# Attention and FFN on one core: scores in one tensor per head, products with v in a slot's fourth quarter, q turned while exp runs, VectorE's FFN work by quarters, the last exp behind the relus

## The chip, the cores and the metric

The kernel runs on 1 core of one Trainium2 chip. The metric is device microseconds of the whole program; three runs of the kernel before are shown.

## The reference

```python
scores = matmul(q, k.T) / 8                       # 8 batches x 8 heads, 576 x 576, head_dim 64
thresh = max(scores, -1) - tau
scores = where(scores >= thresh, scores, -1e9)
attn = exp(scores - max); attn /= sum(attn) + 1e-9
x = matmul(attn, v)                               # heads side by side: (8, 576, 512)
xn = (x - mean(x)) / sqrt(var(x) + 1e-6) * g_ln
out = x + relu(xn @ w_ch1) @ w_ch2                # 512 -> 2048 -> 512, all float32
```

## The kernel before, in words

The attention is cut into **slots**, 9 to a batch (`SLOTS`), 72 in all; `n` counts them, `s` is the slot's place in its batch. A slot holds two heads by 256 rows of q, that is four blocks of 128 x 576 scores. Slots `s` = 0 to 3 take the first 256 rows of the four pairs of heads, `s` = 4 (`HP`) the last 64 rows of all of them, `s` = 5 to 8 the second 256 rows. The **FFN** has 16 groups of 288 tokens, two to a batch. A group has 129 steps: 64 of the first product (16 tiles `p1`, 4 steps each, a relu on ScalarE behind every tile), one for the variance, 64 of the second (4 tiles `p2`, 16 steps each). A step is two matmuls in the program, four in the trace.

The order is written by hand (`manual_schedule`): each engine runs its instructions as the loop over `n` issues them. TensorE gets the slot's products with v (of slot n-2, `values_of`), its scores, and then FFN steps in four **quarters**; `second_part` deals steps to a quarter so that a group ends when the next is `ready`. `at_quarter` puts a call into a later quarter, and `run` makes the calls. `aside` holds VectorE's FFN work (the product of `p2` with `rb`, which frees the tile `p2`; the turning of the finished tile and its store), made by `run_aside`.

In a slot: VectorE takes the maxima (L339, two reduces of two blocks each), ScalarE four exps (L347), VectorE masks and sums (L354, four), GpSimd divides (L360, four). From the second batch on VectorE then turns 32 x 32 blocks (L430) into `et`, SyncE's queue writes `et` to DRAM (`scr`, L436) and `fetch` reads it back as `em` and `er` (L450, L453), the turned weights for the product with v. In the first batch TensorE turns the weights instead (`turn_weights`, L380). At the end of a slot `turn` prepares q and k of the next pair of heads (GpSimd L266, VectorE L269 to L281) and `load_qk` loads the pair after it into the one pair of input tiles. In slots up to the ninth `tick` also converts the FFN's weights, five pieces of work a slot.

PSUM has one tile `sc` of six banks, with the product with v in a corner of the third (`pv`), and two banks that `p1`, `p2`, `mean`, `var` and the turned weights share by turns (`ps_ff`). `product` (L99) issues most matmuls of the FFN.

Of the kernel before, what the change touches and what calls it, by code (L numbers as in the profile page):

```python
# [18 lines left out]
def kernel(  # L19
# [42 lines left out]
    QH = 256  # L62
# [226 lines left out]
    sc = ps_sc.tile([128, 6 * 512], F32, name="sc")  # L289
    pv = sc[:, 1024 + 128 : 1024 + 128 + QH]  # L290

    def block(i):
        return i // 2 * 3 * 512 + i % 2 * S
# [8 lines left out]
    def scores(b, s):  # L302


        if s == HP:
            for hp in range(HP):
                _, kT, qd = turned[b * HP + hp]
                first = block(hp)
                for at, n in span(first, S):
                    o = at - first  # L310
                    product(sc[:, at : at + n], lhsT=qd, rhs=kT[:, o : o + n], start=True, stop=True)
        else:
# [4 lines left out]
            for h in range(2):  # L317
                t = 0
                for j in range(2):
                    first = block(2 * h + j)  # L320
# [3 lines left out]
            for t, h, j, at, n, o in sorted(pieces):  # L324
                r = slice(64 * h, 64 * h + 64)
                nc.tensor.matmul(  # L326
                    sc[:, at : at + n], lhsT=qT[r, half, j * 128 : (j + 1) * 128],
# [3 lines left out]
    blocks = [sc[:, block(i) : block(i) + S] for i in range(4)]  # L331

    def exponentials():
# [40 lines left out]
    def turn_weights(s, es):  # L374

        em, er = turned_tiles()
        for i in range(4):
            tp = ps_ff.tile([128, J, 128], F32, tag="ff", name="tp")
# [32 lines left out]
        return em, er  # L411
# [185 lines left out]
    QUARTERS = 4  # L597
    STEPS = 1 + NK * ND * 2
# [58 lines left out]
    for n in range(NS):  # L657
# [83 lines left out]
```

## Time and profile before

| | |
|---|---|
| median of 3 runs (lowest to highest) | 1831.15 us (1830.4 to 1831.39) |
| the profiled execution: time, span | 1831.4 us, 1829.6 us |
| TensorE busy, mean granted clock | 81%, 0.92 |
| VectorE, ScalarE, GpSimd busy | 45%, 24%, 26% |
| DMA engines, share of the span in SyncE's and ScalarE's hardware queue (q1) | 46.0% |
| the scores of slots n = 0, 9, 16, 70, 71 begin at | 9.6, 243.6, 416.5, 1676.6, 1703.5 us |

The span is from the first to the last instruction; the profiled execution's time is 1.8 us longer. A batch of nine slots takes 209 to 211 us from the second batch on. In the timeline a number in brackets is the time that the engine stood idle before the row, with what ended it.

### The profile page before, as it was taken

Reading aid. Unit: us, or ns where it says so; the run is one execution under the profiler, and the core shown is the slowest. Engines: PE = TensorE matmul, PEld = TensorE weight load, DVE = VectorE, ACT = ScalarE, POOL = GpSimd, SP = SyncE. Lnnn points to the kernel's source line nnn. Section 1 sums busy time; section 2 is a strip of 40 time slices with the busy share of each in tenths; the row PEclk is TensorE's granted clock in tenths of the full one; section 3 lists DMA queues with packets and bytes.
Section 4 is the critical chain, followed back from the end, with each engine's and each line's share of the span. In section 5 each row is a group of like instructions: output and inputs, shape, how many; then the busy total and the mean of one; then the engine's idle time right before and its main releaser. Section 6 shows DMA issues by size and latency. Waiting matters only on the chain.

```text
span 1829.6 us, 29170 instructions
## 1 busy us (share of the span) xinstructions
PE 1489.3 (81%) x11704; PEld 862.9 (47%) x11704; DVE 818.2 (45%) x1380; ACT 444.7 (24%) x810; POOL 476.7 (26%) x735
## 2 busy tenths in 40 slices
PE   3635788888888788888888888888888888887898
PEld 2323444454544444445544544454544545454555
DVE  5557435353543535444454445444454534445210
ACT  3344422213122121322222131312212131221210
POOL 3565322121221212222221222222231222223110
PEclk7777789899999999999999999999999999999999
DMA  6322226444573446545464436645464445634400
GB/s 139 87 73 92 76 44 134 115 115 113 122 171 104 114 107 142 134 116 135 96 154 115 122 104 142 139 112 127 108 156 117 118 109 119 161 104 117 106 12 14
DMA packets 628023, 205.10 MB, mean 112 GB/s; under 512 B 535088, under 2 KB 623792, under 8 KB 627888
## 3 DMA queue, kind: packets, MB, share of 16 engines
q1 hardware_dynamic: 625488, 202.94, 46.0%
q8 instruction: 92, 1.51, 0.3%
q10 hardware_dynamic: 2368, 0.30, 0.1%
q14 instruction: 43, 0.35, 0.1%
q0 software_dynamic: 32, 0.00, 0.0%
HBM read 119.41 MB, written 83.76 MB: 111 GB/s over the span
## 4 chain that ended last, share of the span: by engine, by line
PE 69%; DVE 11%; ACT 10%; issue 4%; POOL 2%; DMA 2%; SPq 2%; ACTq 0%; DVEq 0%; POOLq 0%
PE p L99 49%; PE sc L326 8%; PE sc L478 8%; DVE neg L339 8%; ACT e L347 6%; DVE e L354 2%; PE sc L99 2%; ACT x L494 1%; ACT L347 1%; POOL e L360 1%; ACT hidden L567 1%; DMA er<-scr 1%; SPq L111 1%; DMA stage<-in_moe_w_ch_dram 1%; PE tp L380 1%
## 5 line engine op out<-in xcount | busy, mean ns | idle before, releaser
L99 PE MATMUL p<-xc,w 128*64 128x288 f32 x4096 | 533.4, 419 | 80.4 <-ACT hidden L567 79.0
L99 PE MATMUL p<-hidden,w 128*64 128x288 f32 x4096 | 547.7, 429 | 56.7 <-DVE o L534 30.5
L99 PEld LDWEIGHTS p<-hidden,w 128*64 128x64 f32 x4096 | 309.5, 145 | 283.7 <-issue 40.2
L99 PEld LDWEIGHTS p<-xc,w 128*64 128x64 f32 x4096 | 296.4, 141 | 303.2 <-ACT hidden L567 98.5
L339 DVE TENSOR_REDUCE neg<-sc 128x2 f32<-128x1152 f32 x144 | 188.8, 1353 | 411.5 <-PE sc L326 339.1
L354 DVE SCALAR_TENSOR_TENSOR e<-sc,thr,e 128x576 f32<-128x576 f32 x288 | 218.3, 815 | 212.8 <-ACT e L347 212.7
L360 POOL TENSOR_SCALAR e<-e,den 128x576 f32<-128x576 f32 x288 | 217.2, 770 | 346.7 <-DVE den L358 299.8
L347 ACT ACTIVATE e<-sc,neg 128x576 f32<-128x576 f32 x288 | 189.6, 741 | 324.0 <-DVE neg L339 323.8
L326 PE MATMUL sc<-kT,qT 64*128 64x512 f32 (+3 forms) x1024 | 161.2, 457 | 83.0 <-ACT x L494 37.4
L430 DVE STREAM_TRANSPOSE et<-e 128x1152 f32<-128x1152 f32 x112 | 151.8, 1368 | 56.0 <-POOL e L360 53.9
L567 ACT ACTIVATE hidden<-p 128x288 f32<-128x288 f32 x256 | 102.6, 416 | 305.0 <-PE p L99 305.0
L326 PEld LDWEIGHTS sc<-kT,qT 64*128 64x128 f32 x1024 | 89.3, 200 | 168.0 <-issue 67.6
L494 ACT COPY x<-sc 128x256 f32<-128x256 f32 x64 | 23.8, 372 | 510.7 <-PE sc L478 510.7
L478 PE MATMUL sc<-em,v_in 128*64 128x256 f32 (+1 forms) x1536 | 144.9, 333 | 0.0
L342 POOL TENSOR_SCALAR thr<-neg,low_sb 128x2 f32<-128x2 f32 x144 | 40.8, 283 | 328.8 <-DVE neg L339 328.8
L478 PEld LDWEIGHTS sc<-em,v_in 128*64 128x64 f32 x1536 | 94.0, 140 | 44.0 <-issue 3.6
L535 POOL TENSOR_TENSOR o<-o,x 128x288 f32<-128x288 f32 x64 | 51.0, 796 | 226.1 <-DVE o L534 226.1
L534 DVE TENSOR_TENSOR o<-p,rb 128x288 f32<-128x288 f32 x64 | 28.2, 441 | 139.0 <-PE p L99 138.8
L503 POOL TENSOR_TENSOR sum<-sum,x 128x256 f32<-128x256 f32 (+1 forms) x64 | 31.6, 494 | 182.5 <-ACT x L494 180.0
L380 PE MATMUL tp<-ident,e 128*128 128x128 f32 x144 | 31.4, 379 | 57.8 <-ACT em L389 51.7
L579 DVE RECIPROCAL rb<-rb 128x288 f32<-128x288 f32 x16 | 31.0, 1939 | 73.3 <-ACT rb L578 73.3
L503 POOL TENSOR_TENSOR sum<-x 128x256 f32<-128x256 f32 (+1 forms) x32 | 15.7, 491 | 156.1 <-ACT x L494 135.5
(71 smaller groups left out, 704.1 us busy)
## 6 DMA issues: line engine op xcount, KB each, us to landing
scr<-et SPq DMA_DIRECT2D x224, 288.0 KB, 5.1
em<-scr SPq DMA_DIRECT2D x112, 512.0 KB, 5.0
stage<-in_moe_w_ch_dram SPq DMA_DIRECT2D x22, 512.0 KB, 3.8
q_in<-in_q_dram SPq DMA_DIRECT2D x128, 72.0 KB, 3.3
out_dram<-ot SPq DMA_DIRECT2D x256, 36.0 KB, 1.7
k_in<-in_k_dram SPq DMA_DIRECT2D x124, 72.0 KB, 2.5
v_in<-in_v_dram SPq DMA_DIRECT2D x64, 128.0 KB, 2.6
scr_rest<-et SPq DMA_DIRECT2D x28, 288.0 KB, 4.9
```

Of the source, the lines that this page charges most:

```text
L99: nc.tensor.matmul(out[r], lhsT=lhsT[:, r], rhs=rhs, **flags)
L326: nc.tensor.matmul(sc[:, at : at + n], lhsT=qT[r, half, j * 128 : (j + 1) * 128], rhs=kT[r, o : o + n], start=True, stop=True,)
L339: nc.vector.tensor_reduce(out=neg[:, i : i + 2], in_=sc[:, block(i) : block(i) + 2 * S].rearrange("p (j n) -> p j n", j=2), axis=AXL.X, op ...
L347: nc.scalar.activation(es[:, i], blocks[i], func=AF.Exp, bias=neg[:, i : i + 1])
L354: nc.vector.scalar_tensor_tensor(out=es[:, i], in0=blocks[i], scalar=thr[:, i : i + 1], in1=es[:, i], op0=ALU.is_ge, op1=ALU.mult, accum_o ...
L360: nc.gpsimd.tensor_scalar(out=es[:, i], in0=es[:, i], scalar1=den[:, i : i + 1], scalar2=1.0, op0=ALU.mult, op1=ALU.mult,)
L380: nc.tensor.transpose(tp[:, c], es[:, i, c * 128 : (c + 1) * 128], ident)
L430: nc.vector.transpose(et[:, h].rearrange("p n j c -> p j n c"), es[:, 2 * h : 2 * h + 2].rearrange("p j (n c) -> p j n c", c=32),)
L478: nc.tensor.matmul(dst[64 * h : 64 * h + 64], lhsT=vt[:, c, h, :] if c < J else vr[:, h, :], rhs=rhs, start=(c == 0), stop=(c == J),)
L503: nc.gpsimd.tensor_tensor(out=sums[g][:, cols], in0=x[:, 0, cols] if c == 1 else sums[g][:, cols], in1=x[:, c, cols], op=ALU.add,)
L535: nc.gpsimd.tensor_tensor(out=o, in0=o, in1=groups[g][:, m], op=ALU.add)
L567: nc.scalar.activation(hidden[:, d], p1, func=AF.Relu)
```

## The change

Nothing is added to the arithmetic, and no instruction is taken away. Four things move:

1. The scores lie in two PSUM tiles of three banks, one per head of the slot, so that waits are per head.
2. `exponentials` stops ahead of the fourth exp. The FFN steps of the first quarter, with their relus, are issued ahead of that exp, and `turn` of the next pair and a `run_aside` follow it.
3. `values_of` of slot n-1 is issued at the start of the fourth quarter of slot n (before: of slot n-2 ahead of slot n's scores), and `fetch` moves from the second quarter to the first. `turn_weights` is cut in two.
4. The quarters get shares of 0.6, 1, 1 and 0.6 (`ROOM`); `centre` moves to quarter 1, and `ready` is one quarter earlier.

In SyncE's queue `load_qk` follows the slot's `scr` writes, as before; `fetch` follows these loads, and one store of a finished FFN tile that stood ahead of it in some slots now stands behind it.

```diff
-    sc = ps_sc.tile([128, 6 * 512], F32, name="sc")
-    pv = sc[:, 1024 + 128 : 1024 + 128 + QH]
+    sc = [ps_sc.tile([128, 3 * 512], F32, name=f"sc{i}") for i in range(2)]
+    pv = sc[0][:, 2 * S : 2 * S + QH]
+    blocks = [sc[i // 2][:, i % 2 * S : i % 2 * S + S] for i in range(4)]
...
         for i in range(4):
+            if i == 3:
+                yield es, thr
             nc.scalar.activation(es[:, i], blocks[i], func=AF.Exp, bias=neg[:, i : i + 1])
...
         for i in range(4):
+            if i == 2:
+                yield
             tp = ps_ff.tile([128, J, 128], F32, tag="ff", name="tp")
...
+    ROOM = (0.6, 1.0, 1.0, 0.6)
...
-        return QUARTERS * (b * SLOTS + (HP, 2 * HP)[t] + 2) + 3
+        return QUARTERS * (b * SLOTS + (HP, 2 * HP)[t] + 2) + 2
...
-        owed += ((g + 1) * STEPS - issued) / left if left > 0 else 8
+        owed += ((g + 1) * STEPS - issued) * ROOM[i] / left if left > 0 else 8
...
-        at_quarter(n, 2, centre, g)
+        at_quarter(n, 1, centre, g)
...
         tick(0)
+        scores(b, s)
         run(n, -1)
-        scores(b, s)
-        es, thr = exponentials()
-        tick(1)
+        rest = exponentials()
+        es, thr = next(rest)
         run(n, 0)
         second_part(n, 0)
+        next(rest, None)
+        u = (n + 1) // SLOTS * HP + (n + 1) % SLOTS
+        if (n + 1) % SLOTS < HP and u < len(units):
+            turn(u)
+        run_aside()
+        tick(1)
         run(n, 1)
         second_part(n, 1)
         weights(es, thr)
...
-            at_quarter(n + 1, 1, lambda s=s, scr=scr, box=box: box.append(fetch(s, scr)))
+            at_quarter(n + 1, 0, lambda s=s, scr=scr, box=box: box.append(fetch(s, scr)))
         else:
-            at_quarter(n + 1, 0, lambda s=s, es=es, box=box: box.append(turn_weights(s, es)))
+            made = turn_weights(s, es)
+            at_quarter(n + 1, -1, next, made)
+            at_quarter(n + 1, 0, lambda made=made, box=box: box.append(next(made)))
-        at_quarter(n + 2, -1, lambda b=b, s=s, box=box: values_of(b, s, box[0]))
+        at_quarter(n + 1, 3, lambda b=b, s=s, box=box: values_of(b, s, box[0]))
...
-        u = (n + 1) // SLOTS * HP + (n + 1) % SLOTS
-        if (n + 1) % SLOTS < HP and u < len(units):
-            turn(u)
-            if u + 1 < len(units):
-                load_qk(u + 1)
+        if (n + 1) % SLOTS < HP and u + 1 < len(units):
+            load_qk(u + 1)
+        run(n, 3)
```

The first place is ScalarE's order in slot `s` = 2 of a batch. `x` is the copy of the product with v, `e` the exps, `hidden` the relus, `p_` a tile `p1`. Before:

```order
L494 COPY x<-sc 128x256
L347 ACTIVATE e<-sc,neg 128x576 x4
L567 ACTIVATE hidden<-p_5878 128x288
L578 ACT_TABLE_LOAD
L578 ACTIVATE rb<-var,eps_sb 128x288
```

and now (`sc_150` and `sc_151` are the two heads' tiles):

```order
L348 ACTIVATE e<-sc_150,neg 128x576 x2
L348 ACTIVATE e<-sc_151,neg 128x576
L569 ACTIVATE hidden<-p_5730 128x288
L348 ACTIVATE e<-sc_151,neg 128x576
L569 ACTIVATE hidden<-p_5770 128x288
```

One relu now stands ahead of the fourth exp, and the copy of x no longer stands ahead of the exps.

The second place is VectorE's order in slot `s` = 1, from the maxima to the turned weights (`kT`, `qT`, `q_diag` are `turn`, `xc` is `centre`). Before:

```order
L339 TENSOR_REDUCE neg<-sc 128x2 x2
L354 SCALAR_TENSOR_TENSOR e,den<-sc,thr,e 128x576 x4
L358 RECIPROCAL den<-den 128x4
L540 STREAM_TRANSPOSE ot<-o 128x288
L534 TENSOR_TENSOR o<-p_5503,rb 128x288
L518 TENSOR_TENSOR xc<-x,mean 128x288 x4
L430 STREAM_TRANSPOSE et<-e 128x2x18x32 x2
L269 STREAM_TRANSPOSE kT<-k_in 128x576
L273 STREAM_TRANSPOSE qT<-q_in 128x4x2x32 x2
L281 STREAM_TRANSPOSE q_diag_107<-q_in 64x64 x2
```

and now:

```order
L337 TENSOR_REDUCE neg<-sc_150 128x2
L337 TENSOR_REDUCE neg<-sc_151 128x2
L269 STREAM_TRANSPOSE kT<-k_in 128x576
L273 STREAM_TRANSPOSE qT<-q_in 128x4x2x32 x2
L281 STREAM_TRANSPOSE q_diag_107<-q_in 64x64 x2
L542 STREAM_TRANSPOSE ot<-o 128x288
L520 TENSOR_TENSOR xc<-x,mean 128x288 x4
L354 SCALAR_TENSOR_TENSOR e,den<-sc_150,thr,e 128x576 x2
L354 SCALAR_TENSOR_TENSOR e,den<-sc_151,thr,e 128x576 x2
L358 RECIPROCAL den<-den 128x4
L536 TENSOR_TENSOR o<-p_5591,rb 128x288
L432 STREAM_TRANSPOSE et<-e 128x2x18x32 x2
```

`turn` and `centre` have moved ahead of the masked products, and what `turn` waits for (the loads of k and q) now stands ahead of them too.

The third place is TensorE's order around the end of the same slot; before, the products with v stand next to the scores of slot `s` = 2:

```order
L99 MATMUL p_5585<-hidden,w_15_104 64x288 x2
L478 MATMUL sc<-em,v_in 64x256 x8
L478 MATMUL sc<-er,v_rest_109 64x256 x2
L326 MATMUL sc<-kT,qT 128x512 x2
L326 MATMUL sc<-kT,qT 128x64 x2
```

and now, where 13 steps of the next group's first product stand between them and the scores:

```order
L99 MATMUL p_5591<-hidden,w_15_104 64x288 x2
L480 MATMUL sc_150<-em,v_in 64x256 x8
L480 MATMUL sc_150<-er,v_rest_109 64x256 x2
L99 MATMUL p_5695<-xc,w_0_85 64x288 x2
L99 MATMUL p_5695<-xc,w_1_86 64x288 x2
```

This slot and slot `s` = 6 have no FFN step in their third quarter, since a group ends in the second: the products with v come 16 steps behind the scores in slot 1 and 13 in slot 6 (in both also `mean`), and 21 to 26 steps behind them in the others.

## Rows read from the trace of the kernel before

**Rows 1.** Busy time by stretch: us, length, busy (instructions) by engine, clock, DMA.
```profile
168.50:278.00 109.50, 78.49 (x532) 45.16 (x532) 48.36 (x78) 35.24 (x65) 31.34 (x35) 0.80 0.25 65
...
1467.60:1676.60 209.00, 177.89 (x1440) 102.34 (x1440) 96.31 (x162) 47.51 (x86) 50.63 (x84) 0.95 0.50 122
...
1703.50:1829.60 126.10, 115.34 (x932) 67.35 (x932) 19.48 (x34) 16.72 (x33) 14.37 (x20) 0.97 0.17 38
```

**Rows 2.** The same view, one slot (`s` = 1) of a later batch.
```profile
1123.52:1148.29 24.77, 19.21 (x137) 10.55 (x137) 13.16 (x26) 3.01 (x5) 6.44 (x10) 0.86 0.76 170
```

**Rows 3.** Timeline of TensorE: start, us, instructions, idle before them.
```profile
1035.36 1.23 PE L99 MATMUL mean<-sum,avg_sb 128*64 128x288 f32 x4 [6.41 <-DVE o L534]
1036.34 8.80 PE L99 MATMUL p<-hidden,w 128*64 128x288 f32 x52
...
1084.10 12.22 PE L99 MATMUL p<-xc,w 128*64 128x288 f32 x80 [4.54 <-ACT hidden L567]
...
1135.44 10.21 PE L99 MATMUL p<-hidden,w 128*64 128x288 f32 x64 [5.09 <-DVE o L534]
...
1179.11 10.41 PE L99 MATMUL p<-xc,w 128*64 128x288 f32 x84 [3.27 <-ACT hidden L567]
```

**Rows 4.** Timeline of all engines: a table load, a relu, then one slot (`s` = 0).
```profile
1079.82 1.28 ACT L347 ACT_TABLE_LOAD   x1 [5.21 <-DVE neg L339]
...
1096.43 0.41 ACT L567 ACTIVATE hidden<-p 128x288 f32<-128x288 f32 x1 [1.53 <-PE p L99]
...
1102.86 2.33 PE L326 MATMUL sc<-kT,qT 64*128 64x512 f32 x16 [0.50 <-ACT x L494]
...
1105.12 15.74 PE L99 MATMUL p<-hidden,w 128*64 128x288 f32 x128
...
1105.31 2.62 DVE L339 TENSOR_REDUCE neg<-sc 128x2 f32<-128x1152 f32 x2 [12.10 <-PE sc L326]
...
1108.04 2.63 ACT L347 ACTIVATE e<-sc,neg 128x576 f32<-128x576 f32 x4 [5.23 <-DVE neg L339]
...
1110.78 0.82 DVE L354 SCALAR_TENSOR_TENSOR e<-sc,thr,e 128x576 f32<-128x576 f32 x1 [2.85 <-ACT e L347]
...
1114.13 2.91 POOL L360 TENSOR_SCALAR e<-e,den 128x576 f32<-128x576 f32 x4 [5.83 <-DVE den L358]
1115.64 2.82 DVE L430 STREAM_TRANSPOSE et<-e 128x1152 f32<-128x1152 f32 x2 [1.26 <-POOL e L360]
```

**Rows 5.** The chain of waits, one batch: start, us, work; products with v.
```profile
1120.86 2.21 PE sc L478 x20
```

**Rows 6.** Timeline of all engines: first and last of the turn at that slot's end.
```profile
1118.38 0.74 DVE L269 STREAM_TRANSPOSE kT<-k_in 128x576 f32<-128x576 f32 x1
...
1119.69 0.45 DVE L281 STREAM_TRANSPOSE q_diag<-q_in 64x64 f32<-64x64 f32 x2
```

**Rows 7.** Timeline of SyncE's queue: issues of slot `s` = 0, then of `s` = 5.
```profile
1118.48 4.37 SPq L436 DMA_DIRECT2D scr<-et  x4
...
1127.64 2.12 SPq L111 DMA_DIRECT2D k_in<-in_k_dram  x4
...
1135.30 0.59 SPq L450 DMA_DIRECT2D em<-scr  x1
...
1231.07 4.38 SPq L436 DMA_DIRECT2D scr<-et  x4
...
1241.09 0.59 SPq L450 DMA_DIRECT2D em<-scr  x1
```

**Rows 8.** DMA view: issues, KB each, median us from issue to landing.
```profile
em<-scr SPq DMA_DIRECT2D x112, 512.0 KB, 5.0
...
k_in<-in_k_dram SPq DMA_DIRECT2D x124, 72.0 KB, 2.5
```

**Rows 9.** Timeline of TensorE in the first batch.
```profile
49.15 4.43 PE L326 MATMUL sc<-kT,qT 64*128 64x512 f32 x16 [3.71 <-DVE qT L278]
...
179.12 1.09 PE L380 MATMUL tp<-ident,e 128*128 128x128 f32 x4 [7.72 <-ACT em L389]
```

More of the change, by code (lines that the diff above doesn't have):

```diff
@@ L307, in scores @@
                 _, kT, qd = turned[b * HP + hp]
-                first = block(hp)
+                first = hp % 2 * S
                 for at, n in span(first, S):
                     o = at - first
-                    product(sc[:, at : at + n], lhsT=qd, rhs=kT[:, o : o + n], start=True, stop=True)
+                    product(sc[hp // 2][:, at : at + n], lhsT=qd, rhs=kT[:, o : o + n], start=True, stop=True)
         else:
@@ L319, in scores @@
                 for j in range(2):
-                    first = block(2 * h + j)
+                    first = j * S
                     for at, n in span(first, S):
@@ L326, in scores @@
                 nc.tensor.matmul(
-                    sc[:, at : at + n], lhsT=qT[r, half, j * 128 : (j + 1) * 128],
+                    sc[h][:, at : at + n], lhsT=qT[r, half, j * 128 : (j + 1) * 128],
                     rhs=kT[r, o : o + n], start=True, stop=True,
                 )
-    blocks = [sc[:, block(i) : block(i) + S] for i in range(4)]
     def exponentials():
@@ L346, in exponentials @@
         for i in range(4):
+            if i == 3:
+                yield es, thr
             nc.scalar.activation(es[:, i], blocks[i], func=AF.Exp, bias=neg[:, i : i + 1])
-        return es, thr
     def weights(es, thr):
@@ L410, in turn_weights @@
                 )
-        return em, er
+        yield em, er
     def turn_blocks(s, es):
@@ L622, in second_part @@
         g = issued // STEPS
-        left = ready(g + 1) - at if g + 1 < NG else 0
-        owed += ((g + 1) * STEPS - issued) / left if left > 0 else 8
+        left = sum(ROOM[t % QUARTERS] for t in range(at, ready(g + 1))) if g + 1 < NG else 0
+        owed += ((g + 1) * STEPS - issued) * ROOM[i] / left if left > 0 else 8
         while queue and owed >= 0.5:
@@ L628, in second_part @@
                 queue.pop(0)
-                if left > 1:
+                if left > ROOM[i]:
                     break
@@ L698 @@
         elif n >= SLOTS - 2 and (n + 2) % SLOTS < HP and n < NS - 2:
-            at_quarter(n, 3, load_v, (n + 2) // SLOTS * HP + (n + 2) % SLOTS)
-        run(n, 3)
+            load_v((n + 2) // SLOTS * HP + (n + 2) % SLOTS)
         second_part(n, 3)
@@ L705 @@
         n += 1
-        run(n, -1)
         for i in range(QUARTERS):
```

13 lines of the change are left out of this document (6 added, 7 removed).

## Prediction

> **What bounds the kernel now.** I read the busy time by stretch first. In a settled batch of nine slots TensorE works 177.9 of 209.0 us, at a mean granted clock of 0.95, and no other engine passes half [rows 1]. So a batch is TensorE's own work plus its waits, here 31.1 us; six such batches (n = 16 to 69) take 1260 of the 1829.6 us. TensorE's timeline tells what the waits are [rows 3]: 6.41 us for `mean` and 5.09 for a second product, both for VectorE to free a tile `p2`; 4.54 and 3.27 for a relu on ScalarE (and three like them); and 0.50 in each slot, where the scores wait for the copy of x [rows 4]. The reader should also see what follows a wait. 52 matmuls take 8.80 us behind the wait of 6.41, 64 take 10.21 behind 5.09, 80 take 12.22 behind 4.54 [rows 3]; at the rate of 128 in 15.74 [rows 4], or 0.123 each, they would take 6.4, 7.9 and 9.8. The granted clock has dropped to its lower level (1.2 of 2.4 GHz): the slot with the 5.09 us wait shows 0.86 [rows 2]. With `mean` itself, which takes 1.23 us for four matmuls, that is 3.2 + 2.4 + 2.4 = 8 us a batch. The rest is work: 210 (the mean of the six batches) - 31 - 8 = 171 us.
>
> **What the change takes away.** Slots carry their place `s` in a settled batch; where the whole run is meant I give n. I count time t from the start of a slot's scores, and 0.49 us a step (15.74 / 32).
>
> *Copy of x.* The products with v now have at least four steps of FFN (2.0 us) behind them ahead of the next scores, and the copy needs 0.5: nine times 0.5, 4.5 us, go. If the copy came late, the 0.5 would return.
>
> *VectorE's FFN work.* The `run_aside` behind the first quarter and the new shares let each `p2` be freed at a slot's end or behind the masked products, 6 us or more before its bank is wanted: the 6.41 and 5.09 go, with 5.6 of lost clock. Late next would be the variance's reciprocal, which in one slot in nine delays the maxima by some 0.5 us.
>
> *Relus.* Before, a relu waited for four exps, which end at t = 7.8 [rows 4]. Now the first head's exps start behind the first reduce (t = 3.9), the third waits for the second reduce (t = 5.07) and ends at 5.9, and a relu of 0.41 ends at 6.35. TensorE has two banks, so it waits when it wants the third tile: in slots 2 and 7 it stands from 5.76 (seven steps behind the scores) to 6.35, 0.6 us each. Once a group the exp's table has to be loaded, 1.28 us [rows 4]: slot 8 waits 1.35 (eight steps, 6.26 to 7.6), slot 3 waits 2.75 (six steps, 5.27 to 8.0, with the late maxima). Sum 5.3, in place of 15 and 2.4 of clock. The fourth exp, now behind a relu, ends at about 7.0 and delays only the second head's masked products. Bounds: 0, if relus slip ahead, to 10, if each wait keeps two thirds of its old length.
>
> **What it adds: two new waits.** They lie on DMAs, and the trace of before has no such wait, so I lay them out from the queue's rows.
>
> *q turned while exp runs.* `turn` stands on VectorE ahead of the masked products; `kT` waits for k, loaded behind the previous slot's `scr`. From the start of `scr` to the last k issue is 10.8 us (the four end 1129.76 - 1118.48 = 11.3 behind it) [rows 7], and 2.5 to landing [rows 8]: 13.3. In slot 8 nothing is waited for (its k is long there). Its `turn` takes 1.8 us [rows 6] from t = 5.1, plus some 0.5 for q on GpSimd, so its masked products start at 7.4; 3.35 later GpSimd starts and 4.35 after that `scr` [rows 4, 7]: t = 15.1. Its k lands at 28.4, which is t = 6.6 of slot 0 (slot 8 takes 21.8: 32 steps, scores 2.33, products with v 2.21 [rows 5] and its wait). So slot 0's `turn` and a store's transpose end at 9.2, and its `scr` starts at 17.0. The next k lands at 30.3, t = 10.1 of slot 1 (slot 0 takes 20.2): VectorE waits 5 us there, with `centre` and the masked products queued behind. TensorE does not wait for these; what is late next is `fetch`.
>
> *Products with v.* From the start of `scr` to the issue of the second `em` is 16.8 us [rows 7], and 5.0 to landing [rows 8]: 21.8. So in slot 1 `em` lands at 17.0 + 21.8 - 20.2 = 18.6. TensorE wants it at 2.33 + 16 x 0.49 + 0.6 (`mean`) = 10.8, since slot 1's third quarter is empty: **a wait of 7.8 us**, and 3.2 of clock as behind the 6.41. In slot 6 (no loads; `scr` at t = 13.0 of slot 5, 10.0 to the second `em` [rows 7], 5.0 landing, slot length 17.6) it lands at 10.4 and is wanted at 9.2: 1.2. In slots 0, 2 and 3 I get it 0 to 2 us before it is wanted, in the others 5 or more: 0, bound 6 in all. Together 12.2; bounds 4 (both land 3 us earlier, and the clock stays) to 30 (loads and fetches a third slower).
>
> The landing of 5.0 us has a rival price. The Trainium skill's page SBUF - State Buffer, section on the DMA setup-cost knee, fits about 2 us plus bytes / 436 GB/s, which for 512 KB is an estimate of 3.2. By it the wait in slot 1 would be 6.0, and the whole 12 us less. The measured 5.0 is taken.
>
> **The sum.** A batch: 171 + 5.3 + 12.2 = 188.5, against 210: 21.5 saved, six times, **129 us**. Ahead of that stretch, n = 0 to 15 end at 416 us. In the first batch a slot's scores waited for q (3.71 us idle, [rows 9]) because `turn` stood last; now they follow the product with v: some 5 us for each of n = 1 to 3, 4 for n = 0, 4 each for 4 and 5, 1 for 6 (bound there by the conversion on VectorE), 6 each for 7 and 8, where `em` copies no longer wait for four exps (a wait of 7.72, and 31 of 109.5 us idle, [rows 1, 9]). That is 40; n = 9 to 15, already like the settled ones, give 18. **58 us**, bounds 25 to 75. n = 70 gives 6. The end behind the scores of n = 71 (126.1 us [rows 1]) has 208 FFN steps in place of 217 (4.4 us), a relu wait 3.2 shorter and 2.4 of clock back: **10**. Sum 129 + 58 + 6 + 10 = 203. From the span of 1829.6 that leaves 1626.6, and with the 1.8 us around it **1628 us**; the profiled execution (1831.4) is 0.25 above the median, which I leave.
>
> **The rivals.**
>
> *DMAs a third slower when slots are denser.* For it: the DMA share of slot 1 is already 0.76 [rows 2], and the chain `scr`, k, `turn`, mask, `scr` feeds itself through slots 8, 0, 1 and 2. Against: those four slots get hardly shorter, so the same bytes meet the same room. Then k lands 4.4 us and `em` 7 us later; slots 0 to 3 lose some 13 us more and 2.4 of clock: 15 a batch, over 6.75 batches 104: 1732.
>
> *The waits per head do not come.* If exp of the first head still waited for both reduces, the four relu waits would each be 1.3 longer: 5.2 x 6.75 = 35, 1663. Against: in the new order ScalarE waits for VectorE once per head.
>
> *Slower.* The same chain is the mechanism: VectorE's `turn`, waiting for k in slots 0, 1 and 2, holds back the masked products, hence `scr`, hence the next load and `em`. Each slot would have to lose 7.2 us more to eat the 21.5 a batch: the 13.3 from `scr` to k would have to become 20.5. From there on it is slower than before; at 23, 1831 + 3 x 2.5 x 6 = 1876. For it: nothing but the share of 0.76. Against: it took 11 to 14 us in all such slots of before.
>
> *No gain.* Waits that merely change places would leave 1831; the third and fourth quarters would have to be as full of waits as the first, and no releaser in the rows says so.
>
> **How the numbers follow.** Forecast 0.76, slower DMAs 0.12, waits not per head 0.05, slower 0.04, no gain 0.01, better than all bounds 0.02. Down, the start's better bound (17) with half of the new waits' (8 x 6 / 2 = 24) gives about 1590; up, its worse bound (33) with half of theirs (18 x 6 / 2 = 54) gives 1715. That takes in the second rival but not the first: with all others left out, 0.19. A measurement can tell about 0.2% (3.7 us) from no change. Faster 0.95, same 0.01, slower 0.04.
>
> **What would show it.** Per batch 188 us with a clock of 0.96 or more; in slot 1 a wait of about 8 us of the products with v for `em`; `kT` waiting some 5 us for k in slot 1; no wait for `o` ahead of `mean`, none for the copy of x ahead of the scores; relu waits under 3 us; the scores of n = 9 at about 204. The forecast is wrong if `em` is waited for in most slots, if VectorE's wait for k passes 10 us, or if a batch takes over 200.

## The result and the profile after

The changed kernel takes 1656.9 us (median of 4 runs, 1656.2 to 1659.6) against 1831.3 (4 runs, 1830.4 to 1831.7): ratio 0.9051, 95% interval 0.9035 to 0.9067. It is 174 us faster; the forecast was 203, and the time lies inside the range. The profiled execution took 1659.6 us, its span is 1657.9.

The scores of n = 9, 16, 70 and 71 begin at 215.7, 369.3, 1520.5 and 1541.5 us in the trace after. Against the starts of before this splits the gain along the prediction's sum:

| stretch | forecast saving | measured | how |
|---|---|---|---|
| first batch, n = 0 to 8 | 40 | 27.9 | 243.6 - 215.7 |
| n = 9 to 15 | 18 | 19.2 | 47.1 - 27.9 (n = 16 begins 47.1 sooner) |
| six batches, n = 16 to 69 | 129 | 109.0 | 1260.1 - 1151.2, by the starts to a hundredth |
| n = 70 | 6 | 5.9 | 26.85 - 20.96 |
| behind the scores of n = 71 | 10 | 9.7 | 126.1 - 116.4 |
| sum | 203 | 171.7 | 1829.6 - 1657.9 |

Busy time by stretch, after (columns: window, its length, then busy us and instructions of TensorE, its weight loads, VectorE, ScalarE, GpSimd; granted clock, DMA share, GB/s). The first two rows are the start; the third answers to the settled batch of [rows 1], here six batches at once; then slot s = 1 (its answer of before is [rows 2]), s = 2 and s = 6 of the last of them:

```profile
0.00:215.70 215.70, 131.35 (x864) 80.54 (x864) 136.40 (x229) 98.55 (x182) 111.36 (x135) 0.78 0.40 101
215.70:369.30 153.60, 139.35 (x1142) 83.78 (x1140) 76.92 (x132) 36.89 (x67) 43.39 (x71) 0.97 0.54 125
369.30:1520.50 1151.20, 1059.81 (x8641) 627.88 (x8640) 583.94 (x972) 286.07 (x517) 303.23 (x504) 0.96 0.57 136
1391.67:1422.16 30.49, 22.72 (x159) 13.75 (x157) 13.37 (x26) 5.20 (x9) 6.44 (x10) 0.83 0.67 147
1422.16:1441.61 19.45, 18.25 (x142) 10.26 (x141) 10.43 (x18) 6.50 (x13) 6.53 (x11) 1.00 0.61 139
1498.39:1520.51 22.12, 20.42 (x163) 13.32 (x161) 11.14 (x20) 5.61 (x10) 7.14 (x11) 1.00 0.62 145
```

A batch is 191.9 us (1151.2 / 6), of which TensorE works 176.6 and idles 15.2; before, the same six batches had 179.1 and 30.9 (1074.8 and 185.3 over 1260.1). So half of the idle time went, and 2.5 us of busy time.

TensorE's timeline of one settled batch after, all rows with 0.3 us or more of idle time (in brackets) ahead of them; it answers to [rows 3]:

```profile
1335.38 6.04 PE L99 MATMUL p<-xc,w 128*64 128x288 f32 x48 [0.36 <-ACT hidden L569]
1357.63 4.10 PE L99 MATMUL p<-xc,w 128*64 128x288 f32 x32 [1.16 <-ACT hidden L569]
1409.23 1.08 PE L480 MATMUL sc<-em,v_in 128*64 128x256 f32 x2 [6.84 <-DVE o L536]
1411.24 3.25 PE L480 MATMUL sc<-em,v_in 128*64 128x256 f32 x13 [0.93 <-DMA em<-scr]
1428.39 7.01 PE L99 MATMUL p<-xc,w 128*64 128x288 f32 x56 [0.36 <-ACT hidden L569]
1436.59 1.73 PE L480 MATMUL sc<-em,v_in 128*64 128x256 f32 x13 [0.76 <-DMA em<-scr]
1449.17 9.19 PE L99 MATMUL p<-xc,w 128*64 128x288 f32 x60 [2.18 <-ACT hidden L569]
1509.96 1.73 PE L480 MATMUL sc<-em,v_in 128*64 128x256 f32 x13 [1.70 <-DMA em<-scr]
```

The waits for `mean`, for a second `p2` and for the copy of x are gone. Four of the five waits for a relu are left, all shorter: 1.16 and 2.18 us in s = 8 and s = 3, 0.36 in s = 7 and s = 2; the one in s = 4 is gone. What is new stands in the last quarter: 6.84 + 0.93 = 7.8 us in slot s = 1, 0.76 in s = 2, 1.70 in s = 6.

VectorE in that slot s = 1 (its scores began at 1391.67), and SyncE's queue from slot 0's `scr` on:

```profile
1401.95 0.78 DVE L269 STREAM_TRANSPOSE kT<-k_in 128x576 f32<-128x576 f32 x1 [5.24 <-DMA k_in<-in_k_dram]
...
1405.60 0.80 DVE L354 SCALAR_TENSOR_TENSOR e<-sc,thr,e 128x576 f32<-128x576 f32 x1
...
1406.33 0.81 DVE L354 SCALAR_TENSOR_TENSOR e<-sc,thr,e 128x576 f32<-128x576 f32 x1
...
1407.81 0.81 DVE L354 SCALAR_TENSOR_TENSOR e<-sc,thr,e 128x576 f32<-128x576 f32 x1
```

```profile
1388.33 4.37 SPq L438 DMA_DIRECT2D scr<-et  x4
1392.80 5.09 SPq L111 DMA_DIRECT2D q_in<-in_q_dram  x4
1397.93 2.12 SPq L111 DMA_DIRECT2D k_in<-in_k_dram  x4
...
1404.89 0.38 SPq L452 DMA_DIRECT2D em<-scr  x1
...
1405.89 0.57 SPq L452 DMA_DIRECT2D em<-scr  x1
```

Two things end ahead of these products. The first half of `em`, issued at 1404.89, lands 4.2 us later, at 1409.1 (the shorter of the two landings in the view of the tile `em` for 1385 to 1425):

```profile
DMA to landing us min/median/max: 4.2/4.8/5.3
```

The other end is VectorE's. The products write `pv`, which lies in the tile of the first head's scores. The first two of the four masked products read this tile; they end at 1407.1, 2 us ahead of `em`. The row names VectorE (`o`) because that came last by the profile, but in all six settled slots s = 1 the products start some 0.14 us behind the landing of `em`, and the first head's masked products are done 1.4 to 2.3 us ahead of that landing. So `em` holds TensorE in the changed kernel. Whether VectorE would hold it too if `em` came earlier, the first experiments ask.

### The profile page after: what moved, and what is told of

It reads as the page before. It is cut to its first block, busy times and chain, and to the rows that moved or that the text cites. A ratio compares the mean times of both kernels' runs of the same rounds, so it can differ in the third digit from the quotient of the medians.

```text
span 1657.9 us, 29066 instructions
## 1 busy us (share of the span) xinstructions
PE 1460.1 (88%) x11704; PEld 868.1 (52%) x11704; DVE 827.6 (50%) x1380; ACT 444.9 (27%) x810; POOL 475.8 (29%) x735
## 4 chain that ended last, share of the span: by engine, by line
PE 59%; DMA 9%; DVE 9%; SPq 8%; ACT 7%; POOL 4%; issue 3%; POOLq 0%; ACTq 0%; DVEq 0%
PE p L99 41%; PE sc L480 9%; DMA em<-scr 7%; PE sc L324 5%; DVE neg L337 4%; ACT e L348 4%; SPq L546 3%; POOL e L360 2%; SPq L111 2%; DVE e L354 2%; SPq L438 2%; PE sc L99 2%; ACT L348 1%; ACT hidden L569 1%; DVE rb L581 1%
## 5 line engine op out<-in xcount | busy, mean ns | idle before, releaser
L99 PE MATMUL p<-xc,w 128*64 128x288 f32 x4096 | 545.4, 417 | 30.5 <-ACT hidden L569 28.7
L99 PE MATMUL p<-hidden,w 128*64 128x288 f32 x4096 | 514.6, 408 | 0.0
L99 PEld LDWEIGHTS p<-xc,w 128*64 128x64 f32 x4096 | 320.9, 140 | 231.8 <-ACT hidden L569 52.3
L99 PEld LDWEIGHTS p<-hidden,w 128*64 128x64 f32 x4096 | 291.8, 137 | 197.6 <-issue 1.7
L348 ACT ACTIVATE e<-sc,neg 128x576 f32<-128x576 f32 x288 | 195.3, 741 | 258.5 <-DVE neg L337 258.1
L480 PE MATMUL sc<-em,v_in 128*64 128x256 f32 (+1 forms) x1536 | 179.1, 363 | 75.4 <-DMA em<-scr 49.3
L354 DVE SCALAR_TENSOR_TENSOR e<-sc,thr,e 128x576 f32<-128x576 f32 x288 | 220.1, 814 | 31.0 <-ACT e L348 30.5
L480 PEld LDWEIGHTS sc<-em,v_in 128*64 128x64 f32 x1536 | 105.2, 150 | 140.4 <-DMA em<-scr 34.8
L324 PE MATMUL sc<-kT,qT 64*128 64x512 f32 (+3 forms) x1024 | 154.5, 439 | 23.4 <-DVE e L354 11.0
L575 POOL TENSOR_TENSOR sq<-sq 128x288 f32<-128x288 f32 x48 | 38.4, 801 | 103.0 <-ACT sq L573 100.5
L480 PE MATMUL sc<-er,v_rest 128*64 128x256 f32 (+1 forms) x384 | 63.2, 352 | 0.0
```

Of the source, the lines that this page charges most:

```text
L99: nc.tensor.matmul(out[r], lhsT=lhsT[:, r], rhs=rhs, **flags)
L324: nc.tensor.matmul(sc[h][:, at : at + n], lhsT=qT[r, half, j * 128 : (j + 1) * 128], rhs=kT[r, o : o + n], start=True, stop=True,)
L354: nc.vector.scalar_tensor_tensor(out=es[:, i], in0=blocks[i], scalar=thr[:, i : i + 1], in1=es[:, i], op0=ALU.is_ge, op1=ALU.mult, accum_o ...
L480: nc.tensor.matmul(dst[64 * h : 64 * h + 64], lhsT=vt[:, c, h, :] if c < J else vr[:, h, :], rhs=rhs, start=(c == 0), stop=(c == J),)
```

## The experiments

All start from the changed kernel (1656.9 us) unless said otherwise. "Batch" is a sixth of the stretch from the scores of n = 16 to those of n = 70.

| run | time (us) | ratio to before, interval | n = 16 at | batch | slot s = 1 |
|---|---|---|---|---|---|
| changed kernel | 1656.9 | 0.9051 (0.9035 to 0.9067) | 369.3 | 191.9 | 30.5 |
| e1 loads early | 1603.7 | 0.8753 (0.8727 to 0.8779) | 367.6 | 183.2 | 24 |
| e2 fetch first | 1750.8 | 0.9556 (0.9538 to 0.9574) | 376.0 | 206.0 | 34 to 37 |
| e3 turn back | 1624.7 | 0.8875 (0.8862 to 0.8888) | 373.5 | 185.2 | 27 |
| e4 pv back | 1660.5 | 0.9062 (0.9042 to 0.9081) | 382.8 | 190.0 | 25 |
| e5 loads and v early | 1605.0 | 0.8757 (0.8742 to 0.8772) | 368.9 | 184.1 | 21 to 26 |
| e6 one tensor | 1745.6 | 0.9539 (0.9517 to 0.9560) | 396.6 | 200.7 | 30 |
| e7 exps whole | 1667.3 | 0.9107 (0.9093 to 0.9120) | 367.4 | 193.7 | 29 to 32 |
| e8 FFN back | 1720.4 | 0.9395 (0.9377 to 0.9413) | 375.3 | 199.8 | 26 to 29 |
| e9 loads on ScalarE's queue | 1837.6 | 1.0037 (1.0023 to 1.0052) | 387.2 | 218.2 | 31 to 33 |
| e10 turn in the middle | 1906.2 | 1.0407 (1.0390 to 1.0425) | 403.7 | 227.2 | 37 to 38 |
| e11 conversion later | 1689.7 | 0.9230 (0.9216 to 0.9244) | 402.7 | 191.2 | 30 to 31 |
| e12 stores late | 1604.8 | 0.8736 (0.8711 to 0.8761) | 370.7 | 182.3 | 20 |

### What holds the products with v in slot 1: e1 and e2

e1, the loads behind the turn:

```diff
             turn(u)
+            if u + 1 < len(units):
+                load_qk(u + 1)
...
-        if (n + 1) % SLOTS < HP and u + 1 < len(units):
-            load_qk(u + 1)
         run(n, 3)
```

> One part of the changed kernel is moved: the loads of the next q and k are issued right behind the turn of q, in a slot's first half, and so ahead of the slot's scr on SP's queue. Theory A (the queue): in a batch's slot s=1 the products with v wait because k stands behind scr, and em behind k; both come earlier now (k lands in the slot before, em is issued some 7 us sooner), so the waits there (6.8 + 0.9 us idle, 3.3 of lost clock) go, and small ones in slots 2 and 6: about 11 us a batch, 6.75 batches, 1657 - 74 = 1583, between 1580 and 1600. Rival B (the DMAs are short of room, share 0.67 there): the loads then only push scr back, and the time stays within 1645 to 1665. Rival C (the loads hold the queue while scr waits behind them): scr starts later in slots 8, 0 and 1, em no earlier, and the time is 1665 to 1690.

e2, `fetch` at the end of its own slot, ahead of the loads:

```diff
-            at_quarter(n + 1, 0, lambda s=s, scr=scr, box=box: box.append(fetch(s, scr)))
+            at_quarter(n, 4, lambda s=s, scr=scr, box=box: box.append(fetch(s, scr)))
...
+        run(n, 3)
+        run(n, 4)
         if (n + 1) % SLOTS < HP and u + 1 < len(units):
             load_qk(u + 1)
-        run(n, 3)
```

> In the changed kernel em is fetched at the end of its own slot, behind the slot's products with v and ahead of the loads of q and k, in place of behind those loads in the next slot. Theory D (the prediction's: only em holds the products with v in slot s=1, VectorE's masked products hold nobody on TensorE): em lands there some 6 us sooner, the wait of 6.8 + 0.9 falls to under 2, and the time to about 1657 - 6.75 x 8 = 1603, between 1595 and 1625. Theory M (two ends that lie side by side: in slot 1 the masked products end at 17.0 us behind the scores, em's first half lands at 17.6, and the products with v wait for both, since they write a bank that the masked products read): k now comes some 6 us later, VectorE waits some 11 us for it in place of 5.2, the masked products end at 23, and the wait in slot 1 grows to 12 or 13 us, in spite of an em that is long there. By M the time is 1680 to 1730.

e2 took 1750.8 us: slower than the changed kernel by 94, with an `em` that is there early. Its rows in a slot s = 1 that begins at 1271.5, first SyncE's queue, then VectorE, then TensorE:

```profile
1269.41 4.37 SPq L438 DMA_DIRECT2D scr<-et  x4
...
1278.21 0.38 SPq L452 DMA_DIRECT2D em<-scr  x1
...
1283.90 2.74 SPq L111 DMA_DIRECT2D k_in<-in_k_dram  x4
```

```profile
1289.52 0.78 DVE L269 STREAM_TRANSPOSE kT<-k_in 128x576 f32<-128x576 f32 x1 [12.99 <-DMA k_in<-in_k_dram]
```

```profile
1263.33 3.68 PE L480 MATMUL sc<-em,v_in 128*64 128x256 f32 x16 [3.00 <-DVE e L354]
1294.78 3.68 PE L480 MATMUL sc<-em,v_in 128*64 128x256 f32 x16 [12.57 <-DVE e L354]
1324.11 3.52 PE L480 MATMUL sc<-em,v_in 128*64 128x256 f32 x16 [4.90 <-DVE e L354]
```

`em` is issued 16 us ahead of its use, and the wait grows from 6.8 to 12.6 (12.6 to 15.7 in the six slots), for the masked products (L354), which stand behind 13 us of waiting for k. The same wait now shows in slots 0 and 2 as well, which the expectation had not counted, and it makes the time pass its 1680 to 1730. Theory D falls: **TensorE does wait for VectorE's wait for k**, once `em` is there early enough. It waits for the first head's masked products alone: the products with v start at 1294.78, behind the second of the four (it ends at 1294.7) and ahead of the end of the fourth (1296.2):

```profile
1293.90 0.81 DVE L354 SCALAR_TENSOR_TENSOR e<-sc,thr,e 128x576 f32<-128x576 f32 x1
...
1295.38 0.81 DVE L354 SCALAR_TENSOR_TENSOR e<-sc,thr,e 128x576 f32<-128x576 f32 x1
```

So theory M is right about the wait, and wrong that the two ends lie side by side in the changed kernel: it took the end of the fourth masked product for that of the second.

e1 moves both ends earlier and gains 53 us: VectorE waits for nothing in slot 1 (`kT` follows the reduces at once), `em` is issued at 1171.0, 6.7 us behind the scores (13.2 in the changed kernel), and the wait is 2.34:

```profile
1178.21 2.40 PE L480 MATMUL sc<-em,v_in 128*64 128x256 f32 x10 [2.34 <-DMA em<-scr]
```

It gained less than the 74 of theory A, and its 1603.7 lies just outside the range of 1580 to 1600, because 2.34 and some lost clock stay (granted 0.93 in that slot), and because slot 6 did not get shorter.

### The parts, each undone by itself: e3, e4, e6, e7, e8

e3 puts `turn` and the loads back at the slot's end:

```diff
-        if (n + 1) % SLOTS < HP and u < len(units):
-            turn(u)
         run_aside()
         tick(1)
...
-        if (n + 1) % SLOTS < HP and u + 1 < len(units):
-            load_qk(u + 1)
+        if (n + 1) % SLOTS < HP and u < len(units):
+            turn(u)
+            if u + 1 < len(units):
+                load_qk(u + 1)
```

> One part of the change is undone: q and k are turned at the slot's end again (with the loads behind it as before); all else as in the changed kernel. VectorE no longer waits for k ahead of the masked products. Theory M: both ends in slot s=1 come earlier (masked products 5 to 6 us, scr of slots 8 and 0 and with it em some 3 to 4 us), the wait there falls from 7.7 to about 4, with less lost clock: 5 us a batch less, 30 in six. The first batch loses what the early turn gave there: scores wait for q again in n = 1 to 4 (3.7 us each by the rows of before), 15 to 20 more. Together about 1645, between 1635 and 1660. Rival (the early turn is what carries the gain of the settled batches): a batch takes over 195 us and the time is over 1690.

1624.7 us, 32 faster than the changed kernel, and better than the range: the early turn, as the change places it, is a loss. Slot 1 falls to 27 (its wait to 3.87 + 0.86), slot 2 to 18.1. In the first batch I had written the gain of n = 0 to 3 (19 us) to the early turn. With the turn put back, TensorE does stand before the scores again (n = 2 is shown, n = 3 waits as long),

```profile
45.63 4.42 PE L324 MATMUL sc<-kT,qT 64*128 64x512 f32 x16 [8.32 <-DVE qT L278]
```

but n = 9 begins at 219.5 in place of 215.7: 3.8 us. The waits of n = 1 to 3 sum to 33.8 there and to 27.8 in the changed kernel, where `em`'s copies and the masked products are waited for in place of q.

e4 puts the products with v back ahead of the scores of the second next slot:

```diff
-        at_quarter(n + 1, 3, lambda b=b, s=s, box=box: values_of(b, s, box[0]))
+        at_quarter(n + 2, -2, lambda b=b, s=s, box=box: values_of(b, s, box[0]))
...
+        run(n, -2)
         scores(b, s)
```

> One part of the change is undone: the products with v stand ahead of the second next slot's scores again, in place of in the next slot's last quarter; all else as in the changed kernel. Expected back: the wait of the scores for the copy of x, 0.5 us in each of 9 slots, 4.5 a batch. Expected gone: the products' wait for em (11.9 us a batch, with 3.3 of clock). In its place in slot s=1 TensorE goes on to the first FFN steps of the new group, which need VectorE's centred x, some 3.5 us later than they would be wanted (there is nothing else in the third quarter). Theory A: net 4.5 - 15.2 + 5 = -6 a batch, so this part alone is a loss in the settled batches: about 1620, between 1605 and 1640. Rival E: the products in the last quarter are worth what the copies and the cover of the slot's start are, and without them the time is 1665 to 1700.

1660.5 us, the same as the changed kernel within the noise (the intervals overlap): neither theory. A batch is 1.9 us shorter (190.0), not 6: the waits for x and for `xc` come back as expected, but the products of slot 1, now ahead of slot 3's scores, still wait for `em`:

```profile
1204.93 2.33 PE L324 MATMUL sc<-kT,qT 64*128 64x512 f32 x16 [0.50 <-ACT x L496]
1219.45 2.16 PE L99 MATMUL p<-xc,w 128*64 128x288 f32 x16 [3.80 <-DVE xc L520]
1248.02 0.82 PE L480 MATMUL sc<-em,v_in 128*64 128x256 f32 x2 [1.96 <-DMA em<-scr]
```

and the first batch loses 15.4 (n = 9 at 231.1). So this part is worth its place at the start, and costs a little behind it.

e6 puts both heads' scores into one tensor at the same addresses:

```diff
-    sc = [ps_sc.tile([128, 3 * 512], F32, name=f"sc{i}") for i in range(2)]
+    both_sc = ps_sc.tile([128, 6 * 512], F32, name="sc")
+    sc = [both_sc[:, i * 1536 : (i + 1) * 1536] for i in range(2)]
```

> One part of the change is undone: both heads' scores lie in one tensor of six banks, at the same addresses as before; all else as in the changed kernel. Theory of the prediction (its second rival turned round): the first head's exps now wait for the second head's reduce, so the four relu waits of a batch are each up to 1.3 us longer (2.18 to 3.5 in s=3, 1.16 to 2.5 in s=8, 0 to 1.3 in s=2 and 7), 5.2 a batch, 35 in all, and up to 20 more of lost clock: 1690 to 1712. Rival (waits are kept by region, not by tensor): the same as the changed kernel, 1652 to 1662.

1745.6 us, 89 slower. The relu waits are as expected:

```profile
1230.22 5.79 PE L99 MATMUL p<-xc,w 128*64 128x288 f32 x32 [2.46 <-ACT hidden L570]
1303.10 7.01 PE L99 MATMUL p<-xc,w 128*64 128x288 f32 x56 [1.66 <-ACT hidden L570]
1324.99 7.50 PE L99 MATMUL p<-xc,w 128*64 128x288 f32 x60 [3.46 <-ACT hidden L570]
```

With a second 1.66 in s = 7 they sum to 9.2, against 4.1: each is 1.3 longer, 5.2 in all. The batch grew by 8.8; 2.6 of it is busy time (179.2 against 176.6). What the expectation lacked is that the products with v now wait for the masked products of both heads, though the addresses are the same. In the first batch this takes 4.4 to 4.8 us in each of n = 1 to 5 (n = 3 shown; the fourth masked product ends at 82.8), 23.2 in place of 4.3, and n = 9 begins 17.8 us later:

```profile
82.86 3.75 PE L481 MATMUL sc<-em,v_in 128*64 128x256 f32 x16 [4.75 <-DVE e L355]
```

```profile
80.51 0.81 DVE L355 SCALAR_TENSOR_TENSOR e<-sc,thr,e 128x576 f32<-128x576 f32 x1
...
81.98 0.81 DVE L355 SCALAR_TENSOR_TENSOR e<-sc,thr,e 128x576 f32<-128x576 f32 x1
```

This is the dearest part of the change.

e7 issues all four exps ahead of the relus:

```diff
         for i in range(4):
-            if i == 3:
-                yield es, thr
             nc.scalar.activation(es[:, i], blocks[i], func=AF.Exp, bias=neg[:, i : i + 1])
+        yield es, thr
```

> One part of the change is undone: all four exps are issued ahead of the first quarter's relus; all else as in the changed kernel. Each relu of a first quarter that TensorE waits for ends one exp (0.66 us) later: s=3 from 2.18 to 2.8, s=8 from 1.16 to 1.8, s=2 and s=7 from nothing to 0.5: 2.3 a batch, 16 in all, with 5 more in the first batch where em's copies stand behind the exps: about 1678, between 1665 and 1690. Rival (the waits in slots 2 and 6 for em swallow it): 1655 to 1662.

1667.3 us, 10 slower. The relu waits are 0.99, 1.79, 0.99 and 2.81, 2.5 us more a batch where 2.3 was expected; the batch grew by 1.9, and slot 1 is 0.6 shorter.

e8 undoes the order of the FFN's work:

```diff
-    ROOM = (0.6, 1.0, 1.0, 0.6)
+    ROOM = (1.0, 1.0, 1.0, 1.0)
...
-        return QUARTERS * (b * SLOTS + (HP, 2 * HP)[t] + 2) + 2
+        return QUARTERS * (b * SLOTS + (HP, 2 * HP)[t] + 2) + 3
...
-        at_quarter(n, 1, centre, g)
+        at_quarter(n, 2, centre, g)
...
-        run_aside()
         tick(1)
```

> One part of the change is undone: VectorE's and TensorE's FFN work stands as before (no call of the put-off work behind the first quarter, centre in the third quarter, equal shares of steps, a group ready one quarter later); all else as in the changed kernel. Theory of the prediction: the two waits for VectorE to free a p2 come back (6.4 ahead of mean in s=6, some 5 in s=1), 11.5 a batch with 5.6 of clock, but in s=1 part of it lies under the wait for em and the masked products (6.8): between 8 and 17 a batch, 1657 + 54 to 115: 1711 to 1772. Rival (with the products with v in the last quarter these waits lie beside others): 1655 to 1690.

1720.4 us, 63 slower; the waits for VectorE to free a `p2` are back in both places:

```profile
1263.51 10.91 PE L99 MATMUL p<-hidden,w 128*64 128x288 f32 x64 [8.47 <-DVE o L536]
...
1369.51 1.23 PE L99 MATMUL mean<-sum,avg_sb 128*64 128x288 f32 x4 [3.85 <-DVE o L536]
```

### SyncE's queue and ScalarE's: e5, e9, e10, e12

e5 is e1 with `load_v` moved behind the turn too.

> As the run with q and k loaded behind the turn (1603.7 us), and v's loads move there too, out of the stretch between scr and em. Theory A (the queue): in that run the products with v in slot s=1 still waited 2.34 us for em, which was issued 6.9 us behind scr's last issue (4.8 of it v's loads); without them em waits for scr's landing alone and is issued some 2 us sooner; next late are the masked products (12.3 us behind the scores; wanted at 11). 1 to 2 us a batch in slot 1, with some clock, 0 elsewhere: 1590 to 1600. Rival (em's issue is set by scr's landing and the stores anyway): 1600 to 1607. Both can be told apart only at the slot: 23.9 us long there.

1605.0 us: no gain, the rival. In e1 slot 0's `scr` starts 15.4 us behind the scores and the first `em` is issued 11.3 later; in e5 these are 17.5 and 9.2: `scr` waits behind the loads that were taken from behind it. The batch of 184.1 is from a profiled execution of 1612.9 us, the slowest of e5's five.

e9 issues q and k from ScalarE's queue, at the slot's end: `load_qk(u + 1, (nc.scalar, nc.scalar))`.

> In the changed kernel the loads of q and k stay at the slot's end but are issued by ScalarE's queue in place of SP's, which issues nearly without a break in slots 8, 0, 1 and 2 (scr 4.4, q and k 6.7, v 2.2, em 2.1, stores 4: 19.4 of 20.1 us in slot 0). Theory Q (SP's issue time is the resource in those slots, and so the run with v's loads moved too gained nothing: it put scr 2 us later and em 2 us nearer): k lands a slot early, em waits for scr's landing alone, some 5 us sooner than in the run with early loads; in slot s=1 the masked products (12.3 us behind the scores, wanted at 10.9) end last: slot 1 about 22 us long in place of 23.9, and the time 1585 to 1597. Rival (the 8 issues of 0.5 us hold up relus behind them on ScalarE in slots 8, 1 and 2, about 2 us each with lost clock): 1600 to 1625.

1837.6 us, 181 slower than the changed kernel, which neither theory held. The relus are not what it waits for; SyncE's queue stands still between two loads of v, here in slots 0 and 1:

```profile
1337.62 6.12 SPq L438 DMA_DIRECT2D scr<-et  x4
1344.99 0.39 SPq L125 DMA_DIRECT2D v_in<-in_v_dram  x1
1357.81 0.48 SPq L129 DMA_DIRECT2D v_rest<-in_v_dram  x1
```

`em` is fetched behind them (at 1361.7), and the products with v wait for it 4.5 us in slot 0, 9.3 in slot 1, 11.3 in slot 2 and 6.3 in slot 8. What the second load waited for stands in the trace: it is issued 0.06 us behind the landing of a load of q that ScalarE's queue had issued at 1355.2, in slot 1. The view of SyncE's waits shows such waits 37 times, 381 us in all; the changed kernel has none (columns: us in total, times, longest):

```profile
SPq L125 <- DMA q_in<-in_q_dram: 208.3, 13, 19.8
SPq L129 <- DMA q_in<-in_q_dram: 172.8, 24, 14.5
```

The two loads share no tile. In the trace their landings count on the same semaphore, one of eight that the DMAs of both queues use by turns; no run gave them semaphores of their own, so this last step is read and not tried. So SyncE's queue, with `em` behind the load, waits for the next slot's `turn`, behind which ScalarE's loads of q stand. e10 builds on e9 and moves VectorE's part of the turn behind the masked products; it suffers the same (416 us of these waits), so it decides nothing about the masked products.

> As the run with q and k loaded by ScalarE's queue, and VectorE's part of the turn moved behind the masked products (the scaling of q by GpSimd stays ahead of them). Theory M (the masked products are the last end in slot s=1 once k and em are early): they end 2.4 us sooner there (10.4 us behind the scores), the rest of the wait goes: slot 1 at 20 to 20.5 us, and 7 to 15 us less than the run it is built on: 1575 to 1588. Rival (et is now 1 us later in slots 8, 0 and 1, and em with it, so the wait stays as a wait for em): the same as the run it is built on within 4 us.

e12 is e5 with the output's stores issued behind the next `fetch` and `centre` back behind the masked products.

> As the run with the loads of q, k and v behind the turn (1605.0 us), with two more edits for slot s=1: the output's stores are issued behind the next slot's fetch of em in place of ahead of scr (4 issues, 2.0 us, or 4.4 right behind scr), and centre stands behind the masked products in place of ahead of them (1.5 us on VectorE). Theory Q (SP's order is what sets em there): scr starts some 2 us sooner in slot 0 (at about 15.4 us behind the scores), em's halves land at 9.4 and 10.5 us of slot 1, the masked products end at 10.8, and TensorE wants them at 10.9: slot 1 falls from about 23 to 20 or 21 us, slot 6 from 22.5 to 20.5 or 21.5, its stores too having stood ahead of scr: 3 to 5 us a batch, 1605 - 20 to 34: 1571 to 1585. Rival (em waits for scr's landing whatever stands around it, and scr for the masked products): slot 1 stays at 22 to 24, and the time at 1598 to 1610.

Slot 1 fell as theory Q says, from some 23 to 20 us, and has hardly a wait left. Slots 0, 1 and 2 of one batch:

```profile
1142.74:1162.83 20.09, 20.09 (x167) 11.86 (x165) 11.94 (x22) 3.01 (x5) 6.44 (x10) 1.00 0.63 147
1162.83:1182.89 20.06, 19.75 (x159) 12.70 (x157) 13.26 (x26) 5.20 (x9) 6.44 (x10) 1.00 0.69 149
1182.89:1202.28 19.39, 18.25 (x142) 10.33 (x141) 10.41 (x18) 6.50 (x13) 6.54 (x11) 1.00 0.72 159
```

But the time is that of e1 and e5 (1604.8 beside 1603.7 and 1605.0). Slot 2 went from 18.1 in e1 (18.1 to 22.5 in e5) to between 19 and 23, waiting for `em`: eight stores (5.9 us) now stand ahead of slot 1's loads and push its `scr` back. Slot 6 stayed at 21.6 to 23.9. Among these three runs, then, the queue's order chose which slot waits. What keeps a batch near 182 to 184 us in all three is open; it is not the queue's issues alone, which in e12 fill 12 to 18 us of each of slots 0 to 2.

### The start: e11

```diff
-        ticks = (0, 2) if n < 4 else range(5)
+        ticks = (0, 2) if n < 6 else range(5)
```

> The start, by itself: in the changed kernel the weights' conversion keeps two parts a slot up to n = 5 (it had two up to n = 3 and five from n = 4 on). Theory C (in n = 4 to 6 VectorE's conversion steps, which wait for GpSimd, stand ahead of a slot's maxima and exps, and so hold em's copies: 8.8 + 2.1 us of TensorE's waits in n = 5, 9.0 + 3.9 in n = 6; it is why n = 9 started at 215.7 and not at 204): these waits go, slots n = 4 to 6 are 15 to 20 us shorter, and as TensorE has FFN work enough from n = 7 on, the end comes 8 to 18 us sooner: 1640 to 1650. Rival (the conversion only moves: the FFN of the first group waits for weights, or VectorE is held in n = 6 to 9 instead): 1653 to 1672.

1689.7 us: the first half of theory C is right, its end is wrong. n = 9 begins at 200.0 in place of 215.7, so in n = 4 to 6 it was the conversion that held `em`'s copies. But the FFN then waits for its weights:

```profile
253.23 1.23 PE L99 MATMUL p<-hidden,w 128*64 128x288 f32 x4 [16.34 <-DVE w L230]
```

and n = 16 begins 33 us later than in the changed kernel. The conversion has to be done somewhere ahead of n = 10.

## Why the prediction was right, and where it was 29 us off

**What is taken away** came as written. *Copy of x*: no wait is left in a settled slot. *VectorE's FFN work*: both waits are gone, and e8 shows that this part does it. *Relus*: forecast 5.3 (0.6, 0.6, 1.35 and 2.75 in slots 2, 7, 8 and 3), measured 4.1 (0.36, 0.36, 1.16 and 2.18). e6 and e7 show that waits per head and the split exps carry it. The second rival (no waits per head) has its price confirmed for the relus, 1.3 each; but without waits per head the products with v wait too, so that e6 cost 89 and not 35.

**The new waits.** *Products with v*: forecast 7.8 in slot 1, 1.2 in slot 6, 0 in slots 0, 2, 3; measured in the batch shown 7.8, 1.7, and 0.8 in slot 2. *k*: VectorE was to wait 5 us in slot 1 and waits 5.24. Size and cause are as forecast: in all six slots s = 1 the landing of `em` ends the wait. One sentence beside it was wrong: "TensorE does not wait for these". It does, through the tile that `pv` shares with the first head's scores; e2 shows it with a wait of 12.6. In the changed kernel this stays hidden by 1.4 to 2.3 us, the time by which these masked products are ahead of `em`. That was luck, for the prediction did not count it: whoever had acted on the text and fetched `em` ahead of the loads would have lost 94 us, as e2 did.

*The landing of `em`* is 4.9 us at the median of 112 fetches in the changed kernel, as in [rows 8]. The Trainium skill's page SBUF - State Buffer, section on the DMA setup-cost knee, would give an estimate of 3.2; this trace does not agree.

**The sum, first term**: a batch came to 191.9 in place of 188.5, 3.4 more, 20 us over six. The idle time was near (15.2 against 14.3: 4.1 for relus and some 11 for `em`, in place of 5.3 and 9.0). What was mis-sized is the time lost to the clock behind the waits: busy are 176.6 against 171 + 3.2. Behind the wait in slot 1 it is 2.7 (22.5 busy on the mean of six, where the slot of e12 shown above needs 19.75), near the 3.2. None was counted behind the relu wait of 2.18 in s = 3: the 60 matmuls after it take 9.19 us in five of the six batches, at a mean granted clock of 0.81 in the row below, and 7.50 in the sixth, at 1.00:

```profile
682.37:689.87 7.50, 7.50 (x62) 4.51 (x64) 5.18 (x9) 2.12 (x5) 2.91 (x4) 1.00 0.68 177
1449.17:1458.36 9.19, 9.19 (x62) 5.19 (x64) 5.18 (x9) 2.11 (x5) 2.91 (x4) 0.81 0.32 96
```

That is 1.4 a batch. Slot 2 has 18.3 busy where e1 has 17.6, and one of the six slots s = 6 has 22.1 where the others have 20.2 to 20.4: 0.6 and 0.3 more. With these four taken off, 171.6 are left, so the 171 of work was right.

**The sum, second term**: the first batch saved 27.9 in place of 40. By slot, n = 0 to 8, the forecast was 4, 5, 5, 5, 4, 4, 1, 6, 6 and the saving 4.1, 0.5, 4.1, 2.6, 9.5, 3.9, -7.2, 5.9, 4.4. Two steps failed. One is "1 for 6 (bound there by the conversion on VectorE)": slot 6 got 7 us longer, because the conversion's work, no longer hidden behind other waits, had caught up; e11 shows the cause, with a slot 6 of 24.5 us in place of 33.0. The other is "some 5 us for each of n = 1 to 3": the three gave 7.2 in place of 15, since `em`'s copies and the masked products are waited for there in place of q. That the turn carries these is wrong too: e3 gives it 3.8 in the whole batch, while e4 gives the products' move 15.4, all of it in n = 4 and 5. The extra 5.5 in n = 4 made up for part of the miss, by luck.

**The rivals.** *DMAs a third slower*: `em` landed as before, `scr` took 5.6 against 5.1; it did not come. *Slower* through k: the distance from the start of `scr` to the landed k was 13.6 in the slot shown (1401.95 - 1388.33), against the 20.5 that it needed. Its mechanism is real, and its price about right: in e2 the distance is 20.1 (1289.52 - 1269.41) and a batch takes 206.0, near the 210 of before. *No gain* is excluded by the interval.

**The parts.** Undone one by one they cost 89 (one tensor), 63 (FFN's order), 10 (last exp), 4 (products with v, within the noise), and -32 (turn): the change is three gains, a part that pays at the start and costs behind it, and one loss. It is the turn's place ahead of the masked products with the loads left behind `scr` that loses; with the loads moved behind the turn (e1) the kernel takes 1603.7 us, 53 less than the changed kernel and 228 less than before.

## What to carry to other kernels

When a step is moved ahead on an engine, move the transfers that it needs with it (e1), or it takes its own wait along and puts it in front of everything queued behind. Before moving a transfer, ask what else the waiting work needs, and when that ends: the next end can be 2 us behind the one you remove, and the move itself can put it off (e2). The engine that a profile names beside a wait is the one that came last by the profile; here it names VectorE in three of six slots where `em`'s landing ended the wait, so compare the ends themselves. And where several slots hang on one DMA queue, look at every slot after a new order: e1 took 53 us out of the queue's order, but in e5 and e12 the wait only went from one slot to another.

## What the runs showed of the hardware

The largest surprise is e9: with the same eight loads a slot on ScalarE's queue, SyncE's queue stood 12.4 us between two loads of v (1345.4 to 1357.8), and the kernel lost 181 us. Two queues are not independent when DMAs on one wait for landings on the other, here 381 us in all. The second is that one and the same wait is followed by either clock: behind a relu wait of 2.18 us, 60 matmuls took 7.50 us in one of the changed kernel's six settled batches and 9.19 in the others, 7.50 in five of e1's six and in all six of e3's. What decides it was not tried. The third is that a matmul waits for another engine's reads of other columns of the tile that it writes: behind the second masked product with two tiles (e2), behind the fourth with one tile at the same addresses (e6). Whether the program's own synchronisation asks for this wait or the chip needs it, no run tells.
